# A linear-attention and feed-forward block whose hand-written order and PSUM banks are replaced, tile 1 normalised first and tiles 4 and 5 loaded between the halves of the keys' weight

## The chip, the cores and the metric

The kernel runs on one core of a Trainium2 chip. The core has a matrix engine (TensorE; PE in the profile, its weight loads PEld), a vector engine (VectorE, DVE), a scalar engine (ScalarE, ACT), GpSimd (POOL) and a queue for transfers (SyncE, SP). The metric is the device time of one execution in microseconds (us).

## The reference

The input is one sequence of 2048 rows of 512 bf16 numbers. A pre-normalised linear attention with 32 heads of 16 columns is added to it, and then a pre-normalised feed-forward block with relu of width 1792.

```
h  = x + A(layernorm(x))           # A: linear attention
h2 = h + B(layernorm(h))           # B: relu(h @ w1) @ w2

q, k, v = heads of (x @ wqkv)
phi(t)  = where(t > 0, t + 1, exp(t)) + 1e-6
kv      = sum over s of phi(k)[s, d] * v[s, e]
z       = sum over s of phi(k)[s, d]
o       = (phi(q) @ kv) / (phi(q) @ z + 1e-6)
A       = o.reshape(S, D) @ wo
```

## The kernel before

The 2048 rows are 16 tiles of 128 rows (0 to 15), and four tiles make a chunk of 512 rows (0 to 3). Nothing is scheduled by a compiler: the string `ORDER` is a list of words, the last lines of the kernel read them from left to right, and each word calls one function `op_<name>` with the numbers behind it. An engine runs its instructions in the order in which the words issue them, so the one list is the order of each of the five queues. Where a word on one engine needs the result of another, it waits for it, and everything behind it on that engine waits too.

PSUM has eight banks of 512 f32 columns per partition. The last number of a word of TensorE names the bank that it writes; a later word that writes the same bank waits until the engines that read it are through. `K.4.0` is the keys' product of tile 4 into bank 0.

The words that matter here, in the order in which a tile goes through them:

- `lx` loads tiles of x, `lk`, `lq`, `lv`, `lo`, `l1`, `l2` load weights (lines 201 and 204, SP). `lk.0.2` and `lk.2.2` are the two halves of the keys' weight, 256 KB each; a load of two tiles of x is 256 KB too.
- `S`, `A` (lines 237 and 238, VectorE): statistics of a tile and their sum. `R` (lines 243 and 244, ScalarE): 1/sqrt(variance + eps) as a logarithm and an exponential, of one tile or of several. `N` (line 262, VectorE): the normalised tile into `h_nat`.
- The normalised tile is transposed into `lnT`, in one of two ways. `T` does it on TensorE (line 281) and `E` copies the result out of PSUM on ScalarE (line 291): tiles 0 to 3. `X` does it by a transposing DMA from SP (line 302): tiles 4 to 15. An X needs only its N.
- `K` (line 310): the keys' product, four matmuls of 512 columns, each with a quarter of the weight. `K.t.b.0.2` is its first half, which needs only `lk.0.2`, and `K.t.b.2.2` its second. `F` and `U` (lines 328 and 331, ScalarE) take exp and relu out of PSUM; `M` (line 335, VectorE) clips, `D` (line 338, VectorE) adds, which gives phi(k). `W` does relu and sum in one.
- `G` (line 362): normalised tile times phi(k), summed over all 16 tiles in banks 4 to 7. `za`, `zf`, `z`, `zc`, `zh` make z. `gA` copies G's sum out on ScalarE (line 395), `kv`, `kx`, `m`, `mA` make the matrix that stands for kv and the output weight.
- `Q`, `qF`, `qU`, `qM`, `qD`, `qW`: the same as K to W for the queries of a chunk.
- `dn`, `dnl`, `dnx`: the denominators of a chunk and their reciprocals (line 472, ScalarE). `dt` transposes a tile of these by a DMA (line 491, SP) into `rd`; one tile in each of the first two chunks (2 and 6) goes through TensorE instead (`rt`, then `rv` or `re`). `dm` (line 495, VectorE) multiplies, which needs all four tiles of the chunk.
- `h` (line 505): the attention's output of a tile; `hD` (line 511) adds x. `s`, `a`, `r`, `n`, `x` (`t`, `e` for tile 2) normalise and transpose again.
- `p` (line 521), `pA`, `pD` (lines 527, 532): first feed-forward product and its relu. `f` (line 541) the second, `fo` (line 549) the last sum, `fd` (line 556) the store.
- `warm` and `warmf` (lines 215, 221): matmuls on zeros, whose result nobody reads.

Around the change, the list is this. SP first issues the loads of x and of the keys' weight, which wait for nothing, and then the transposes of tiles 4 to 15, each of which waits for its N. TensorE starts with zeros, transposes tiles 0 to 3 and makes K of them; from G.0 on it goes from K to G to Q without a break in the list. VectorE and ScalarE feed it.

Of the kernel before, what the change touches and what calls it, by code (L numbers as in the profile page):

```python
# [23 lines left out]
A.12 A.13 G.1 R.12.2 K.6.2 K.9.1 M.4.2 S.10 F.6.2 N.12 D.4.2 S.11 A.10 U.6.2 X.8 M.6.2 N.13 G.4 X.12 K.8.0 A.11
R.10.2 S.14 D.6.2 G.5 G.6 X.13 N.10 N.11 S.15 F.8.2 M.8.2 X.11 A.15 U.8.2 A.14 D.8.2 R.14.2 G.7 za.2 za.4 K.12.0
G.9 K.13.1 N.15 N.14 X.10 lq.2.2 K.11.3 F.12.2 K.10.2 M.12.2 U.12.2 F.10.2 masks X.15 X.14 lv.0.2 lv.2.2 l1.0.2
U.10.2 za.6 D.12.2 M.10.2 G.8 za.8 D.10.2 Q.0.1.1 Q.0.0.0 qF.0.0.2 qU.0.0.2 za.10 G.12 K.14.2 K.15.3 Q.0.2.0
za.12 Q.0.3.1 G.13 F.14.2 G.11 qF.0.2.2 l2.10.4 qM.0.0.2 M.14.2 W.14.2 zf.12 G.10 qD.0.0.2 qM.0.2.2 G.14
qU.0.2.2 lo.0.2 z.3.1.14 z.2.1.14 G.15 z.1.1.14 z.0.1.14 qD.0.2.2 zc gA.0.2 gA.2.2 Q.1.0.2 zh dn.0.1 Q.1.1.3
dnl.0 kv.2.7 lo.2.2 kv.1.7 kv.3.7 dnx.0.2.2 qF.1.0.2 kv.0.7 l2.3.4 dnx.0.0.2 Q.1.2.0 l1.2.2 rt.2.6 kx qM.1.0.2  # L30
Q.1.3.1 qF.1.2.2 m.0.4 m.1.5 rv.2 Q.3.1.7 qW.1.0.2 m.3.6 Q.2.3.2 dt.3 qM.1.2.2 mA.0.2 qW.1.2.2 dt.0 dt.1 m.2.5
Q.2.1.4 dn.1.0 mA.2.2 dm.0.0.2 Q.2.2.1 dm.0.2.2 dnl.1 dnx.1.2.2 h.3.6 dnx.1.0.2 h.1.5 rt.6.3 hD.3 qF.2.2.2 dt.7
s.3 re.6 h.0.0 dt.4 qU.2.2.2 hD.1 dt.5 a.3 hD.0 s.1 s.0 a.1 qM.2.2.2 a.0 Q.3.0.6 Q.2.0.3 n.3 h.2.5 n.0 dm.1.0.2
Q.3.3.1 x.3 dm.1.2.2 qF.3.0.2 hD.2 n.1 s.2 Q.3.2.0 qU.2.0.2 qF.2.0.2 h.5.2 h.6.3 a.2 qU.3.0.2 qM.2.0.2 h.4.7 n.2
qF.3.2.2 x.0 qD.2.0.2 t.2.5 qD.2.2.2 hD.4 x.1 hD.6 h.7.4 dn.2.6 hD.5 hD.7 e.2 dnl.2 qM.3.0.2 p.0.0.5 dnx.2.2.2
p.0.13.7 p.0.1.6 p.0.8.2 p.0.9.3 dnx.2.0.2 qD.3.0.2 s.4 l2.7.3 p.0.11.4 pA.0.0.2 dt.11 l2.0.3 dt.9 dt.10 r.0.4
qM.3.2.2 qW.3.2.2 s.6 dt.8 p.0.12.6 s.7 pD.0.12.2 p.0.3.1 p.0.2.0 pA.0.8.2 dn.3.2 p.0.5.7 dnl.3 p.0.4.6 a.7
dm.2.0.2 pA.0.2.2 dnx.3.0.2 dnx.3.2.2 dm.2.2.2 pD.0.4.2 h.9.0 h.8.5 p.0.6.6 p.0.7.7 dt.13 dt.12 s.5 dt.14
p.0.10.3 hD.8 dt.15 s.8 a.6 pD.0.6.2 a.4 pA.0.10.2 n.6 f.1.1.0.7 hD.9 n.7 f.1.1.7.7 s.9 dm.3.0.2 dm.3.2.2 h.11.7
a.5 n.5 h.12.2 h.15.6 h.14.4 fo.1 h.10.5 hD.11 f.0.7.0.7 hD.12 x.6 a.8 h.13.1 a.9 f.3.3.0.7 f.3.3.7.7 x.7 hD.15  # L40
n.4 hD.14 f.0.7.7.7 x.4 f.2.0.0.7 hD.13 fo.3 x.5 p.1.0.6 s.12 s.11 n.8 hD.10 fo.0 p.1.1.7 a.11 fd.0 p.1.5.3 s.10
pD.1.0.2 f.2.0.7.7 a.12 n.12 n.9 s.14 p.1.4.2 n.11 p.1.8.4 fo.2 p.1.3.1 r.4.4 a.10 a.14 p.1.13.7 p.1.2.0
pD.1.4.2 n.10 x.10 x.11 s.13 p.1.7.2 p.1.9.5 p.1.12.6 a.13 pD.1.2.2 s.15 a.15 pD.1.8.2 n.14 pD.1.12.2 p.1.6.1
# [548 lines left out]
```

## Time and profile before

| | |
|---|---|
| time, median of 3 runs | 170.09 us (170.05 to 170.57) |
| span of the profiled execution, first to last instruction | 168.8 us, of 2286 instructions |
| last matmul of that execution ends | 166.14 us after the span's start |
| DMA | 15.49 MB, mean 92 GB/s |

The runs that were timed are other executions than the one that was profiled; for that one the page has the span, to which 1.25 us are missing up to the median.

The page gives for each engine the time in which it was busy. A matmul is shown from its start to a modelled end, and the next one starts before that end; so matmuls that follow each other at full pace look busy throughout, and a short wait between two of them can be hidden in such an overlap. What a group of equal matmuls takes from its start to the start of the next group shows it. The timeline merges neighbouring instructions of one line: start, time from the first start to the last end, engine, line, operation, count, and in brackets the idle time of the engine ahead of it, with what ended it. "Landing" of a DMA counts from its issue to the moment at which all of it has arrived.

### The profile page before, as it was taken

To read this page: it belongs to the slowest core of one execution; us is meant where nothing else is said; L and a number is where in the kernel's file an instruction comes from. 1 tells how busy PE (TensorE), PEld (TensorE's weight loads), DVE (VectorE), ACT (ScalarE), POOL (GpSimd) and SP (SyncE) were. 2 spreads that over 40 slices of the span, in tenths; PEclk is the share of its full clock that TensorE was granted. 3 is DMA by queue.
4 is the path that set the end of the run, shared out by engine and by line. 5 is a ranking of instruction groups with operands and counts; after the bars stand their busy time and mean duration, and the time that the engine had idled before them with its cause. 6 is when DMAs were issued, how large, how long until landed. Compare 5 with 4: busy or idle time off the path is not lost.

```text
span 168.8 us, 2286 instructions
## 1 busy us (share of the span) xinstructions
PE 163.1 (97%) x855; PEld 78.0 (46%) x871; DVE 104.4 (62%) x205; ACT 65.1 (39%) x97; POOL 4.8 (3%) x21
## 2 busy tenths in 40 slices
...
DMA packets 30491, 15.49 MB, mean 92 GB/s; under 512 B 23184, under 2 KB 29328, under 8 KB 30480
## 3 DMA queue, kind: packets, MB, share of 16 engines
...
q8 instruction: 7, 0.11, 0.3%
...
HBM read 7.86 MB, written 2.10 MB: 59 GB/s over the span
## 4 chain that ended last, share of the span: by engine, by line
PE 85%; DVE 7%; DMA 4%; issue 1%; SPq 0%
PE bk L541 29%; PE bk L521 28%; PE bk L505 8%; PE bk L318 8%; PE bk L362 6%; PE bk L310 4%; DVE st L237 3%; DMA x_nat<-in_A_x_dram 2%; DMA lnT<-h_nat 2%; DVE h_nat L262 2%; PE bk L459 1%; DVE eb L335 1%; PE bk L403 1%; PE bk L415 1%; SPq L201 0%
## 5 line engine op out<-in xcount | busy, mean ns | idle before, releaser
L541 PE MATMUL bk<-w_sb,at 128*128 128x512 bf16 (+2 forms) x247 | 50.1, 355 | 0.3
L521 PE MATMUL bk<-lnT,w_sb 128*128 128x512 bf16 x219 | 50.0, 379 | 0.3
L527 ACT ACTIVATE at<-bk 128x1024 bf16<-128x1024 f32 x14 | 14.2, 1023 | 57.4 <-PE bk L521 57.4
L541 PEld LDWEIGHTS <-at 128*128 128x128 bf16 x252 | 23.6, 98 | 25.4 <-ACT at L527 0.3
L549 DVE SCALAR_TENSOR_TENSOR gT<-bk,rstd,h_nat 128x512 bf16<-128x512 f32 (+2 forms) x18 | 12.2, 689 | 35.7 <-PE bk L541 35.6
L521 PEld LDWEIGHTS <-w_sb 128*128 128x128 bf16 x224 | 21.8, 98 | 25.8
L532 DVE TENSOR_SCALAR at<-bk 128x1024 bf16<-128x1024 f32 x14 | 17.1, 1218 | 12.8 <-PE bk L521 12.6
L328 ACT ACTIVATE eb<-bk 128x1024 bf16<-128x1024 f32 (+1 forms) x18 | 16.6, 928 | 6.6 <-PE bk L310 4.8
L310 PE MATMUL bk<-wk_sb,lnT 128*128 128x512 bf16 x63 | 15.3, 380 | 0.4 <-ACT lnT L291 0.3
L505 PE MATMUL bk<-m_sb,pqs 128*128 128x512 bf16 x63 | 15.4, 380 | 0.1
L318 PE MATMUL bk<-lnT,wq_sb 128*128 128x512 bf16 x61 | 15.1, 379 | 0.1
L362 PE MATMUL bk<-at,h_nat 128*128 128x512 bf16 x55 | 13.5, 379 | 0.1
L331 ACT ACTIVATE rb<-bk 128x1024 bf16<-128x1024 f32 (+1 forms) x14 | 12.5, 904 | 0.3 <-PE bk L310 0.3
L511 DVE TENSOR_TENSOR h_nat<-bk,x_nat 128x512 bf16<-128x512 f32 x16 | 10.5, 680 | 2.9 <-PE bk L505 2.9
L237 DVE BATCH_NORM_STATS2 st<-x_nat 128x6 f32<-128x512 bf16 x16 | 10.8, 680 | 2.4 <-DMA x_nat<-in_A_x_dram 2.4
L239 DVE BATCH_NORM_STATS2 st<-h_nat 128x6 f32<-128x512 bf16 x16 | 10.7, 683 | 0.1
L310 PEld LDWEIGHTS <-lnT 128*128 128x128 bf16 x64 | 6.0, 98 | 8.4 <-ACT lnT L291 1.0
L362 PEld LDWEIGHTS <-h_nat 128*128 128x128 bf16 x64 | 6.2, 98 | 7.4 <-issue 0.2
L505 PEld LDWEIGHTS <-pqs 128*128 128x128 bf16 x64 | 5.9, 98 | 7.9 <-DVE pqs L495 1.8
L318 PEld LDWEIGHTS <-wq_sb 128*128 128x128 bf16 x64 | 5.9, 98 | 6.4
L472 ACT ACTIVATE wk_sb<-ld 128x1024 bf16<-128x1024 f32 x8 | 8.1, 1050 | 0.1
L335 DVE TENSOR_SCALAR eb<-eb 128x1024 bf16<-128x1024 bf16 (+1 forms) x18 | 6.8, 383 | 0.9 <-ACT eb L328 0.9
...
## 6 DMA issues: line engine op xcount, KB each, us to landing
...
x_nat<-in_A_x_dram SPq DMA_DIRECT2D x3, 256.0 KB, 4.6
...
wk_sb<-in_A_wqkv_dram SPq DMA_DIRECT2D x2, 256.0 KB, 4.3
wq_sb<-in_A_wqkv_dram SPq DMA_DIRECT2D x2, 256.0 KB, 4.9
```

Source lines behind the costliest of these rows:

```text
L237: op_S = lambda t: nc.vector.bn_stats(out=st[:, t, :], in_=x_nat[:, t, :])
L310: nc.tensor.matmul(bk[:, b, :], lhsT=lnT[c][:, kd, j * P : (j + 1) * P], rhs=wk_sb[:, kd, :], start=(kd == 0), stop=(kd == KD - 1),)
L318: nc.tensor.matmul(bk[:, b, :], lhsT=wq_sb[:, kd, j * P : (j + 1) * P], rhs=lnT[c][:, kd, :], start=(kd == 0), stop=(kd == KD - 1),)
L328: nc.scalar.activation(out=buf(eb, kind, i, n), in_=bank(at_bank[kind, i], n), func=ACT.Exp)
L331: nc.scalar.activation(out=buf(rb, kind, i, n), in_=bank(at_bank[kind, i], n), func=ACT.Relu)
L362: nc.tensor.matmul(bk[:, KD + kd, :], lhsT=ln_nat[:, t, kd * P : (kd + 1) * P], rhs=pk(t)[:, 0, :], start=(t == 0), stop=(t == NT - 1),)
L505: nc.tensor.matmul(bk[:, b, :], lhsT=pqs[:, (c * KD + jb) % NQ, j * P : (j + 1) * P], rhs=m_sb[:, jb, :], start=(jb == 0), stop=(jb == KD ...
L521: nc.tensor.matmul(bk[:, b, cols], lhsT=w1_sb[:, kd, f * P : (f + 1) * P], rhs=lnT[c][:, kd, cols], start=(kd == 0), stop=(kd == KD - 1),)
L527: nc.scalar.activation(out=acts[c % 2][:, f : f + n, :], in_=bank(at_bank["p", c, f], n), func=ACT.Relu)
L532: nc.vector.tensor_scalar(out=acts[c % 2][:, f : f + n, :], in0=bank(at_bank["p", c, f], n), scalar1=0.0, scalar2=None, op0=ALU.max,)
L541: nc.tensor.matmul(bk[:, b, 0 : w * P], lhsT=acts[c % 2][:, f, j * P : (j + 1) * P], rhs=w2_sb[:, f, k * P : (k + w) * P], start=(f == 0), ...
L549: nc.vector.scalar_tensor_tensor(out=o_t[:, t % NO, cols], in0=bk[:, at_bank["f", t, k], 0 : w * P], scalar=rstd2[:, t : t + 1], in1=h_nat ...
```

## The change

Only the string `ORDER` is other. It has the same number of words of every kind, and the same instructions come out, in another order on each engine and with other bank numbers. The first and the last line of it, before and after:

```diff
-const lx.0.1 lx.1.1 warmf.4.3 warm.1.3 S.0 table A.0 R.0.1 S.1 lx.2.2 lk.0.2 warm.1.3 N.0 A.1 S.2 R.1.1 lk.2.2
...
-f.15.5.0.14.2.1 fd.13 fd.14 fd.15.0.2 fo.15.2.1 fd.15.2.1
+lx.0.1 lx.1.1 lx.2.2 lk.0.2 lx.4.2 lk.2.2 lx.6.2 lx.8.4 lv.2.2 table const warmf.4.5 S.0 A.0 S.1 A.1 R.0.1 N.0 R.1.1
...
+f.15.5.0.14.3.1 fo.15.3.1 fd.15.3.1 f.15.4.0.14.2.1 fo.15.2.1 fd.15.2.1
```

As two lines are missing at the head of the file, a line of the kernel after stands two numbers lower than the same line before.

**VectorE, the start of the program.** First the kernel before, from the first statistics on. BN_STATS is S, BN_AGGR is A, TENSOR_SCALAR from x_nat is N.

```order
L237 BN_STATS st<-x_nat 128x6
L238 BN_AGGR mv<-st 128x2
L237 BN_STATS st<-x_nat 128x6
L262 TENSOR_SCALAR h_nat<-x_nat,mv,rstd 128x512
L238 BN_AGGR mv<-st 128x2
L237 BN_STATS st<-x_nat 128x6
L238 BN_AGGR mv<-st 128x2
L237 BN_STATS st<-x_nat 128x6
L238 BN_AGGR mv<-st 128x2
L262 TENSOR_SCALAR h_nat<-x_nat,mv,rstd 128x512 x3
L237 BN_STATS st<-x_nat 128x6 x2
```

The same place after:

```order
L235 BN_STATS st<-x_nat 128x6
L236 BN_AGGR mv<-st 128x2
L235 BN_STATS st<-x_nat 128x6
L236 BN_AGGR mv<-st 128x2
L260 TENSOR_SCALAR h_nat<-x_nat,mv,rstd 128x512 x2
L235 BN_STATS st<-x_nat 128x6
L236 BN_AGGR mv<-st 128x2
L235 BN_STATS st<-x_nat 128x6
L260 TENSOR_SCALAR h_nat<-x_nat,mv,rstd 128x512
L236 BN_AGGR mv<-st 128x2
L235 BN_STATS st<-x_nat 128x6 x2
```

Tile 1 is normalised right behind tile 0 and no longer behind the statistics of tiles 2 and 3; tile 3 comes next, and tile 2 last, behind the statistics of tiles 4 and 5. On TensorE one matmul on zeros that stood ahead of tile 0's transposes goes to a place behind them, tile 1's transposes come ahead of K.0, and tile 3's stand between K.0's halves.

**SP, from the first load to the last transpose of h_nat.** Before (lnT_82, lnT_83, lnT_84 are the chunks 1, 2 and 3 of lnT; a row with x2 or x4 stands for that many DMAs):

```order
L201 DMA x_nat<-in_A_x_dram 128x512 x2
L201 DMA x_nat<-in_A_x_dram 128x1024
L204 DMA wk_sb<-in_A_wqkv_dram 128x2x512 x2
L201 DMA x_nat<-in_A_x_dram 128x1024 x2
L201 DMA x_nat<-in_A_x_dram 128x2048 x2
L204 DMA wq_sb<-in_A_wqkv_dram 128x2x512
L302 DMA_TRANSPOSE lnT_82<-h_nat 128x4x128 x4
L302 DMA_TRANSPOSE lnT_83<-h_nat 128x4x128 x2
L302 DMA_TRANSPOSE lnT_84<-h_nat 128x4x128 x2
L302 DMA_TRANSPOSE lnT_83<-h_nat 128x4x128 x2
L204 DMA wq_sb<-in_A_wqkv_dram 128x2x512
L302 DMA_TRANSPOSE lnT_84<-h_nat 128x4x128 x2
```

After, from the first half of the keys' weight on:

```order
L202 DMA wk_sb<-in_A_wqkv_dram 128x2x512
L199 DMA x_nat<-in_A_x_dram 128x1024
L202 DMA wk_sb<-in_A_wqkv_dram 128x2x512
L199 DMA x_nat<-in_A_x_dram 128x1024
L199 DMA x_nat<-in_A_x_dram 128x2048
L202 DMA wv_sb<-in_A_wqkv_dram 128x2x512
L199 DMA x_nat<-in_A_x_dram 128x2048
L300 DMA_TRANSPOSE lnT_82<-h_nat 128x4x128 x2
L202 DMA wq_sb<-in_A_wqkv_dram 128x2x512
L300 DMA_TRANSPOSE lnT_82<-h_nat 128x4x128 x2
L202 DMA wq_sb<-in_A_wqkv_dram 128x2x512
L300 DMA_TRANSPOSE lnT_83<-h_nat 128x4x128 x2
```

Tiles 4 and 5 of x are loaded between the two halves of the keys' weight. Both halves of the queries' weight now stand between transposes, and half of the values' weight stands ahead of the last four tiles of x. Behind these rows the transposes of chunks 3, 2 and 3 follow, two each, then the remaining loads without one between the later transposes; before, two parts of w2 stood among the transposes of the reciprocals.

**TensorE, in the stretch from tile 6's keys to tile 12's.** In words, since the rows there read alike: before, K.6 K.9 G.4 K.8 G.5 G.6 G.7 K.12; after, K.6 G.4 G.5 K.8 K.9 G.6 K.13 K.12, with tile 8 transposed ahead of tile 9 and tile 13 ahead of tile 12.

More of the change, by code (lines that the diff above doesn't have):

```diff
@@ L24 @@
[L24 to L43, printed above, removed]
@@ new lines @@
+N.1 warm.1.4 T.0.1 E.0 warm.1.7 T.1.3 K.0.4.0.2 S.3 A.3 R.3.1 S.2 N.3 A.2 E.1 R.2.1 masks S.4 S.5 A.4 A.5 N.2 T.3.0
+K.0.4.2.2 E.3 F.0.1 R.4.2 U.0.1 K.1.3.0.2 K.1.3.2.2 warm.1.1 T.2.1 K.3.0 E.2 K.2.2.0.2 K.2.2.2.2 F.3.1 S.6 N.5 M.0.1
+N.4 D.0.1 S.7 M.3.1 A.7 A.6 lx.12.4 X.5 X.4 lq.2.2 U.3.1 R.6.2 U.2.1 F.2.1 U.1.1 F.1.1 D.3.1 S.9 N.7 S.8 A.9 M.2.1 A.8
+R.8.2 N.6 D.2.1 M.1.1 N.9 G.0 G.3 K.5.1 K.4.0 F.4.2 U.4.2 D.1.1 N.8 S.12 M.4.2 S.13 A.12 D.4.2 A.13 X.7 X.6 lq.0.2 X.8
+X.9 R.12.2 G.2 G.1 K.7.2 K.6.1 F.6.2 U.6.2 S.15 N.13 X.13 A.15 S.10 A.10 M.6.2 N.12 D.6.2 S.11 A.11 R.10.2 S.14 N.10
@@ new lines @@
+A.14 N.11 X.12 G.4 G.5 K.8.0 K.9.1 G.6 K.13.3 K.12.2 G.7 F.8.2 R.14.2 U.8.2 U.12.2 F.12.2 za.2 N.15 N.14 M.8.2 D.8.2
+Q.0.1.1 Q.0.0.0 qF.0.0.2 qU.0.0.2 X.10 X.11 X.15 X.14 lo.2.2 l2.3.4 lv.0.2 lo.0.2 l2.0.3 l2.7.3 l1.0.2 l2.10.4 l1.2.2
+K.10.2 K.11.3 za.4 M.12.2 za.6 D.12.2 za.8 G.9 F.10.2 U.10.2 M.10.2 D.10.2 za.10 K.15.1 K.14.0 G.8 F.14.2 M.14.2 za.12
+W.14.2 qM.0.0.2 G.12 Q.0.3.3 Q.0.2.2 G.13 G.10 G.14 G.11 qF.0.2.2 qU.0.2.2 zf.12 z.2.2.14 z.1.2.14 z.3.2.14 z.0.2.14
+G.15 gA.0.2 qD.0.0.2 zc zh qM.0.2.2 qD.0.2.2 Q.1.0.3 gA.2.2 dn.0.1 dnl.0 dnx.0.2.2 Q.1.1.4 kv.3.2 kv.2.2 kv.0.2 kv.1.2
@@ new lines @@
+Q.1.3.1 Q.1.2.0 qF.1.0.2 dnx.0.0.2 kx qM.1.0.2 qW.1.0.2 dt.3 dt.0 dt.1 qF.1.2.2 m.0.6 m.1.7 Q.2.3.2 mA.0.2 rt.2.3
+m.2.5 Q.3.1.4 m.3.6 qM.1.2.2 qW.1.2.2 rv.2 dm.0.0.2 mA.2.2 Q.2.1.7 dn.1.3 Q.2.2.1 dnl.1 dnx.1.0.2 dnx.1.2.2 qF.2.2.2
+qU.2.2.2 dm.0.2.2 h.3.5 hD.3 h.0.3 h.1.0 s.3 hD.0 hD.1 s.0 s.1 a.0 a.3 n.0 n.3 a.1 n.1 rt.6.5 Q.2.0.6 h.2.2 Q.3.3.1
+Q.3.0.3 Q.3.2.0 dt.5 dt.7 dt.4 qF.2.0.2 re.6 qU.2.0.2 dm.1.0.2 dm.1.2.2 h.4.5 h.5.6 h.6.7 hD.2 s.2 a.2 qM.2.0.2 n.2
+qU.3.0.2 qF.3.0.2 qF.3.2.2 t.2.4 qD.2.0.2 qM.2.2.2 hD.6 qD.2.2.2 h.7.2 hD.7 qM.3.0.2 hD.4 x.3 x.0 x.1 e.2 qM.3.2.2
@@ new lines @@
+qD.3.0.2 qW.3.2.2 p.0.3.4 dn.2.7 p.0.2.3 pA.0.2.2 r.0.4 dnl.2 dnx.2.0.2 p.0.6.2 p.0.9.5 p.0.8.4 dn.3.1 pA.0.8.2
+dnx.2.2.2 p.0.7.3 hD.5 s.5 s.6 pD.0.6.2 p.0.10.6 p.0.4.4 p.0.5.5 p.0.1.3 p.0.0.2 s.7 a.6 n.6 s.4 a.4 dt.8 dt.9 dt.11
+dt.10 a.7 pD.0.4.2 a.5 n.7 dm.2.0.2 dm.2.2.2 n.5 p.0.11.7 p.0.12.5 dnl.3 pA.0.0.2 pA.0.10.2 dnx.3.0.2 dnx.3.2.2 r.4.4
+f.0.4.0.7 h.8.1 p.0.13.6 pD.0.12.2 n.4 h.10.3 h.11.0 hD.11 f.1.2.0.7 hD.10 s.10 f.0.4.7.7 f.2.7.0.7 dt.13 dt.14 dt.12
+dt.15 dm.3.0.2 a.10 dm.3.2.2 h.13.6 s.11 hD.8 hD.13 a.11 s.13 x.5 x.7 f.1.2.7.7 fo.1 fd.1 x.4 x.6 h.12.0 h.15.3 a.13
```

22 lines of the change are left out of this document (10 added, 12 removed).

## The prediction

> **What bounds the kernel now.** I read the page's busy times and its chain of work, and then the busy times of stretches.
>
> ```profile
> PE 163.1 (97%) x855; PEld 78.0 (46%) x871; DVE 104.4 (62%) x205; ACT 65.1 (39%) x97; POOL 4.8 (3%) x21
> PE 85%; DVE 7%; DMA 4%; issue 1%; SPq 0%
> ```
>
> ```profile
> 0.00:12.13 12.13, 10.07 (x43) 5.71 (x44) 8.71 (x27) 7.66 (x20) 4.81 (x21) 1.00 0.71 238
> 12.13:49.33 37.20, 36.84 (x225) 17.80 (x228) 32.24 (x67) 27.05 (x39) 0.00 (x0) 1.00 0.68 167
> ```
>
> In the stretches the columns are length, then busy time and count of PE, PEld, DVE, ACT and POOL, granted clock, DMA share and GB/s. TensorE makes 85% of the chain and is busy nearly throughout behind 12.13 us (36.84 of the next 37.20). The change adds and removes no instruction, so only three things can move: when TensorE's unbroken work begins, how long it stands still afterwards, and what lies behind its last matmul. The first stretch, with 2 us of 12 idle, is a chain of VectorE, ScalarE and TensorE.
>
> The pace of unbroken matmuls is in the chain, and the standstills in the timeline:
>
> ```profile
> 129.81 10.14 PE bk L521 x47
> ```
>
> ```profile
> 19.94 1.03 PE L362 MATMUL bk<-at,h_nat 128*128 128x512 bf16 x4
> 21.09 0.55 PEld L310 LDWEIGHTS <-lnT 128*128 128x128 bf16 x4 [0.63 <-DMA lnT<-h_nat]
> 21.10 1.04 PE L310 MATMUL bk<-wk_sb,lnT 128*128 128x512 bf16 x4
> 48.93 0.54 PE L459 MATMUL bk<-zhd,pqT 128*128 128x8 bf16 x16
> 50.25 2.07 PE L505 MATMUL bk<-m_sb,pqs 128*128 128x512 bf16 x8
> 69.81 1.89 PE L521 MATMUL bk<-lnT,w_sb 128*128 128x512 bf16 x8
> 71.62 2.07 PE L505 MATMUL bk<-m_sb,pqs 128*128 128x512 bf16 x8
> ```
>
> 10.14 / 47 gives 0.216 us for a matmul and 0.863 for a group of four. G.4 at 19.94 should end its issue at 20.80, but K.8 starts at 21.10, when X.8 has landed: 0.30 lost. Eight matmuls at full pace take 1.89 (the row at 69.81); the two rows of h take 2.07, so 0.18 is lost in each. Ahead of the first, the small matmuls of dn.1 end their issue at about 49.33 and Q.2.2 would at 50.19, so 0.06 is lost before 50.25; ahead of the second it is 71.62 - (69.81 + 1.73) = 0.08. Together 0.30 + 0.24 + 0.26 = 0.80; the records have little else, so a new order can win **about 0.8 us** behind G.0. The rest has to come from the front.
>
> **The front, step by step.** The rows, in the order in which the walk uses them:
>
> ```profile
> 3.94 0.66 DVE L237 BATCH_NORM_STATS2 st<-x_nat 128x6 f32<-128x512 bf16 x1
> 4.63 0.41 DVE L262 TENSOR_SCALAR h_nat<-x_nat,mv,rstd 128x512 bf16<-128x512 bf16 x1
> 4.82 1.06 PE L215 MATMUL bk<-m_sb 128*128 128x512 bf16 x2
> 4.96 0.18 DVE L238 BATCH_NORM_AGGREGATE mv<-st 128x2 f32<-128x6 f32 x1
> 5.17 0.29 ACT L243 ACTIVATE rstd<-mv,eps 128x1 f32<-128x1 f32 x1 [0.57 <-DVE mv L238]
> 5.49 0.20 ACT L244 ACTIVATE rstd<-rstd 128x1 f32<-128x1 f32 x1
> 5.60 0.70 DVE L237 BATCH_NORM_STATS2 st<-x_nat 128x6 f32<-128x512 bf16 x1 [0.47 <-DMA x_nat<-in_A_x_dram]
> 5.67 0.63 PE L281 MATMUL bk<-ident,h_nat 128*128 128x128 bf16 x4
> 6.34 0.60 ACT L291 ACTIVATE lnT<-bk 128x512 bf16<-128x512 bf16 x1 [0.64 <-PE bk L281]
> 6.99 1.05 PE L310 MATMUL bk<-wk_sb,lnT 128*128 128x512 bf16 x4 [0.26 <-ACT lnT L291]
> 8.24 1.28 DVE L237 BATCH_NORM_STATS2 st<-x_nat 128x6 f32<-128x512 bf16 x2
> 9.43 2.75 PE L310 MATMUL bk<-wk_sb,lnT 128*128 128x512 bf16 x12
> 12.13 1.02 PE L362 MATMUL bk<-pk_lo,h_nat 128*128 128x512 bf16 x4
> ```
>
> A result passes to another engine in about 0.04 us (T.0 ends at 6.30, E.0 starts at 6.34), and VectorE overlaps neighbours by some 0.09 (two S in 1.28).
>
> Tile 0: S.1 ends at 4.60 as before, A.1 now follows, and N.0 runs 4.73 to 5.14, 0.1 later than before. But T.0 stood behind two matmuls on zeros, which issue every 0.43 us (4.82 to 5.67 for two); with one it goes off at 5.25, E.0 runs 5.91 to 6.51, and K.0's first half 6.57 to 7.00. That is 0.42 earlier. Tile 1: A.1 ends at 4.82, R.1 at 5.38 (0.52 from the first start to the last end), N.1 at 5.82, so T.1 fits in ahead of K.0. Tile 3: S.3 5.74 to 6.43, A.3, R.3 to 7.21, N.3 7.25 to 7.65, T.3 at 7.70, and K.0's second half at 7.93 to 8.36. Its weight has moved behind 256 KB of x.
>
> ```profile
> 2.18 0.95 SPq L204 DMA_DIRECT2D wk_sb<-in_A_wqkv_dram  x2
> wk_sb<-in_A_wqkv_dram SPq DMA_DIRECT2D x2, 256.0 KB, 4.3
> ```
>
> The halves were issued from 2.18 and 2.66 and landed 4.3 later, at 6.5 and 7.0; one more place of the same size in the queue is 0.5 to 0.7, so the second lands by 7.7. TensorE is then busy with T.3, which hides it; without that cover it costs what it lands after 7.9.
>
> E.1 is done at 7.72 and K.1 takes 8.36 to 9.22. Tile 2 is the late one: S.4, S.5, A.4, A.5 are ahead of it on VectorE, N.2 runs 9.07 to 9.47, T.2 9.52, K.3 9.75 to 10.61 meanwhile; E.2 waits on ScalarE behind U.0 and ends at 10.70, K.2 takes 10.76 to 11.62. D.0 is ready at 11.26. So **G.0 starts at 11.62 in place of 12.13: 0.51 us won**.
>
> **From G.0 to h.** After G.0, G.3 needs D.3, which VectorE has at 12.58: 0.14 lost. The next points are the transposing DMAs of tiles 4 to 15.
>
> ```profile
> 10.85 14.66 SPq L302 DMA_TRANSPOSE lnT<-h_nat  x10
> lnT<-h_nat SPq DMA_TRANSPOSE x12, 2.5
> ```
>
> ```profile
> 19.27 1.02 ACT L328 ACTIVATE eb<-bk 128x1024 bf16<-128x1024 f32 x1 [0.80 <-PE bk L310]
> 20.34 0.42 DVE L335 TENSOR_SCALAR eb<-eb 128x1024 bf16<-128x1024 bf16 x1
> ```
>
> Issue occupies SP for about 1.2 us of the 2.5 to landing. By the same walk X.5 goes off at 10.44 (before 10.85), X.4 at 11.75 and lands at 14.25, where K.4 wants it at 14.35. X.8 is issued at 16.6 and is wanted at 20.4, so the 0.30 of before is gone even with a load of 256 KB ahead of it. X.9 lands at 20.4 to 21.2 by how much that load holds it up, and is wanted at 21.2: I put 0.1 there. The tight one is X.12. K.6 ends at 18.84, R.12 is ahead of F.6, F.6 ends at 20.12 (1.02), M.6 waits for S.10 and takes 0.42 to 20.88, then comes N.12 to 21.20. X.12 is issued at 21.23 and lands at 23.7; K.12 wants it at 23.85 to 23.95. I count nothing for it, with 0.15 to spare.
>
> Then a chain of waits runs from the last G to h.3:
>
> ```profile
> 39.44 1.02 PE L362 MATMUL bk<-at,h_nat 128*128 128x512 bf16 x4
> 40.07 1.94 ACT L395 ACTIVATE gT<-bk 128x1024 bf16<-128x1024 f32 x2 [2.15 <-PE bk L362]
> 42.35 1.06 ACT L472 ACTIVATE wk_sb<-ld 128x1024 bf16<-128x1024 f32 x1
> 46.53 1.76 SPq L491 DMA_TRANSPOSE rd<-wk_sb  x1
> 49.50 1.29 DVE L495 TENSOR_TENSOR pqs<-pqT,rd 128x1024 bf16<-128x1024 bf16 x2 [1.02 <-DMA rd<-wk_sb]
> ```
>
> gA, dnl, dnx, one qF, the second dnx, two dt, dm: ScalarE, SP and VectorE do them in the same order before and after, from the last G's second matmul on. TensorE's arrival at h.3 moves by -0.51 (front), -0.30 (X.8), +0.14 (G.3) and +0.10 (K.9): 0.57 earlier. The last G, which starts the chain, moves by the same and by +0.20, since two of the four z, which stood behind it, now stand ahead of it (eight small matmuls, 0.1 us): 0.37 earlier, and dm with it. So the stop at h.3 grows from 0.24 to **0.44**. Further on, p.0.3 wants x.1 and e.2 at the moment at which, by the walk, both get there, as dn.2 no longer stands ahead of it: 0.05. At the second stop (h.8 in place of h.9) the chunk's multiplications are there 0.6 before h: its 0.26 go. From chunk 1's p on, every bank is free and every relu done 0.2 us or more ahead, or at the same distance as before.
>
> The end: before, the last group of f is followed by one sum and one small store.
>
> ```profile
> 166.18 0.35 DVE L549 SCALAR_TENSOR_TENSOR gT<-bk,rstd,h_nat 128x128 bf16<-128x128 f32 x1 [0.30 <-PE bk L541]
> ```
>
> After, the same sum and store end it, and the store ahead of it is issued 0.8 earlier: no change.
>
> Sum: front 0.51, standstills of before 0.80 won, standstills of after 0.14 + 0.10 + 0.44 + 0.05 = 0.73 lost: **0.58 us less**. Made against the profiled execution this is a span of 168.2 after 168.8; the median of the timed runs, 170.09, stands 1.25 above that span, and I keep that distance: 169.5.
>
> **The rivals.** *X.12 comes late, and the kernel becomes slower.* Two transposes of before landed late, and the DMA view of two windows, that of X.8's issue and that of X.13's, has their times; in the window behind X.13's issue (22.8 to 22.9 us) stands a packet that is not the kernel's:
>
> ```profile
> lnT<-h_nat SPq DMA_TRANSPOSE x1, 3.4
> lnT<-h_nat SPq DMA_TRANSPOSE x1, 4.1
> q8 instruction: 1, 0.02, 54.8%
> ```
>
> X.13 was issued at 21.1 and took 4.1 instead of 2.5 while 16 KB of instructions were fetched through one of the same DMA engines; it was not wanted soon. After, X.12 is issued at 21.23, and K.12 wants it at 23.9. At 4.1 it lands at 25.3: 1.4 lost, which makes 169.5 + 1.4 = 170.9. It makes the kernel slower than before where the landing takes more than about 3.3. Against it: the fetch follows TensorE's progress, which may come past it a little earlier or stand in front of K.12 until X.12 is there. The Trainium skill ("Runtime: NRT & Kernel Launch", section on instruction fetch) says that the sequencer refills its instructions in blocks of 16 KiB, 256 instructions, through a DMA queue of its own; the packet above is such a block, and by that rule it comes at the same count of TensorE's instructions after, beside X.12, with this rival's 170.9 as the result.
>
> *The gain is eaten at one tight place.* A transpose that lands 0.9 late, as X.8 did (3.4), at K.12 (0.15 to spare), K.9 or p.0.3 costs about 0.7: 170.2, no difference.
>
> *The stops vanish.* If the reciprocals' DMAs run without the delay that they had before (the issue at 46.53 took 1.76 us in place of 1.2, which is 0.56 of the chain), h.3 does not stop: 169.1, and 168.8 if K.9 and G.3 do not either.
>
> *The front does not get earlier*, because N.2, now last of four, or the second half of the weight holds K.2 up to 12.1: 170.0.
>
> **How the numbers follow.** The forecast (169.1 to 169.9) gets 0.42, the late X.12 at its full price 0.17, the gain eaten 0.21, no stops 0.12, no earlier front 0.08. The measurement tells about 0.3%, 0.5 us, from no change, so faster means below 169.58: no stops, and somewhat more than half of the forecast and a little of the others where a row was read 0.1 too dear, 0.44 in all. Slower means above 170.6: the late X.12 and a few of the eaten gains, 0.19. The rest, 0.37, is the same. The range leaves out a tenth at each end: 168.7 to 171.0.
>
> **What would show it.** Right: G.0 in the timeline near 11.6, K.0 in two pieces with T.3 between them, G.3 with a short wait for D.3, no wait for a DMA at K.8, the first h stopped for DVE by about half a microsecond, h.8 not stopped. Wrong: an idle time of TensorE ahead of a group of K from 23 us on with a DMA as its releaser, a first G after 11.9, or a wait among the p and f, where I found none.

## The result, and the profile after

| | before | after |
|---|---|---|
| time, median | 170.09 us (170.0 to 170.57, 5 runs) | 171.54 us (171.1 to 172.61, 5 runs) |
| ratio, 95% interval | | 1.0086, 1.0064 to 1.0107 |
| span of the profiled execution | 168.8 us | 169.7 us |

The kernel became slower by 0.9%, where 0.3% faster was forecast; its time lies above the range. The page of the changed kernel, its busy times and its chain of work, and the busy times of the same two stretches:

```profile
PE 162.5 (96%) x856; PEld 77.4 (46%) x871; DVE 105.2 (62%) x205; ACT 64.5 (38%) x97; POOL 4.7 (3%) x21
...
PE 83%; DVE 8%; DMA 4%; ACT 2%; issue 1%
```

```profile
0.00:11.79 11.79, 9.59 (x43) 5.07 (x44) 8.36 (x26) 7.51 (x19) 4.73 (x21) 1.00 0.73 243
11.79:49.33 37.54, 35.90 (x206) 16.96 (x209) 32.24 (x67) 25.80 (x38) 0.00 (x0) 1.00 0.67 185
```

The front did get shorter (G.0 at 11.79 in place of 12.13). Behind it TensorE is idle for 37.54 - 35.90 = 1.64 us where it was idle for 0.36; at an equal clock, so this is waiting and not a slower engine. The timeline of TensorE from K.8 on shows where (L308 is K, L360 is G; all lines are two lower than before):

```profile
20.56 1.03 PE L308 MATMUL bk<-wk_sb,lnT 128*128 128x512 bf16 x4
21.86 1.04 PE L308 MATMUL bk<-wk_sb,lnT 128*128 128x512 bf16 x4 [0.27 <-DMA lnT<-h_nat]
22.73 1.03 PE L360 MATMUL bk<-at,h_nat 128*128 128x512 bf16 x4
23.59 1.03 PE L308 MATMUL bk<-wk_sb,lnT 128*128 128x512 bf16 x4
25.83 0.81 PE L308 MATMUL bk<-wk_sb,lnT 128*128 128x512 bf16 x3 [1.21 <-DMA lnT<-h_nat]
26.47 0.81 PE L360 MATMUL bk<-at,h_nat 128*128 128x512 bf16 x3
```

The rows are K.8, K.9, G.6, K.13, K.12 (of which one matmul's record is missing) and G.7. At 0.863 for a group, K.9 should start at 20.56 + 0.86 = 21.42 and starts 0.43 later; from K.13's start to G.7's two groups lie, 1.73, and it takes 2.88, so **1.16 us are lost at K.12**. Both wait for a DMA that writes lnT, a transpose. The DMA view, in windows 0.1 us wide, has the causes: the first row is the window of X.12's issue at 21.2, the others are windows at 20.4 and at 23.1 (queue, packets, MB, share of time).

```profile
lnT<-h_nat SPq DMA_TRANSPOSE x1, 4.3
...
q14 instruction: 1, 0.01, 19.3%
...
q8 instruction: 1, 0.02, 79.9%
```

X.12 landed 4.3 us after its issue, not 2.5. While it was in flight, 16 KB of instructions were fetched (23.13 to 24.41 us in the packet's record); X.9, which landed 3.4 after its issue, had an 8 KB packet in it (20.46 to 20.77). The trace keeps sixteen completions for each DMA, as many as the page counts DMA engines. Fifteen of X.12's came 2.27 to 2.43 us after its issue and one at 4.31; of X.9's, fifteen came by 2.53 and one at 3.43. So one of the sixteen parts of each transfer was late, and the others were on time.

Against before's profile, by starts of TensorE's groups: G.0 0.33 earlier; K.8's wait of 0.30 gone; G.3 0.11, K.9 0.43 and K.12 1.16 new; a wait of 0.16 in dn.0 new, the 0.24 at the first h gone; 0.21 at the first p new, the 0.26 at the second h gone. That adds up to 0.94, and the last group of f starts 0.90 later, 166.10 after 165.20.

### The profile page after: what moved, and what is told of

Same layout as the page of the kernel before. It is cut to its first block, busy times and chain, and to the rows that moved or that the text cites. A ratio compares the mean times of both kernels' runs of the same rounds, so it can differ in the third digit from the quotient of the medians.

```text
span 169.7 us, 2286 instructions
## 1 busy us (share of the span) xinstructions
PE 162.5 (96%) x856; PEld 77.4 (46%) x871; DVE 105.2 (62%) x205; ACT 64.5 (38%) x97; POOL 4.7 (3%) x21
## 4 chain that ended last, share of the span: by engine, by line
PE 83%; DVE 8%; DMA 4%; ACT 2%; issue 1%
PE bk L539 28%; PE bk L519 28%; PE bk L503 8%; PE bk L316 8%; PE bk L360 5%; DVE st L235 4%; DMA lnT<-h_nat 3%; PE bk L308 3%; DVE h_nat L260 1%; DMA x_nat<-in_A_x_dram 1%; PE bk L457 1%; DVE mv L236 1%; DVE at L336 1%; DVE eb L333 1%; ACT rb L329 1%
## 5 line engine op out<-in xcount | busy, mean ns | idle before, releaser
L519 PE MATMUL bk<-lnT,w_sb 128*128 128x512 bf16 x219 | 49.5, 379 | 0.3
L308 PE MATMUL bk<-wk_sb,lnT 128*128 128x512 bf16 x63 | 15.6, 380 | 1.5 <-DMA lnT<-h_nat 1.5
L503 PE MATMUL bk<-m_sb,pqs 128*128 128x512 bf16 x62 | 15.3, 379 | 0.1
L241 ACT ACTIVATE rstd<-mv,eps 128x2 f32<-128x2 f32 (+2 forms) x14 | 4.1, 295 | 25.7 <-DVE mv L238 19.6
L360 PE MATMUL bk<-at,h_nat 128*128 128x512 bf16 x55 | 13.5, 379 | 0.1
L308 PEld LDWEIGHTS <-lnT 128*128 128x128 bf16 x64 | 5.7, 98 | 9.2 <-DMA lnT<-h_nat 2.9
L360 PEld LDWEIGHTS <-h_nat 128*128 128x128 bf16 x64 | 6.2, 98 | 7.4 <-issue 0.2
L503 PEld LDWEIGHTS <-pqs 128*128 128x128 bf16 x64 | 6.2, 98 | 7.3 <-DVE pqs L493 0.4
```

The lines of the kernel that those rows point to most:

```text
L308: nc.tensor.matmul(bk[:, b, :], lhsT=lnT[c][:, kd, j * P : (j + 1) * P], rhs=wk_sb[:, kd, :], start=(kd == 0), stop=(kd == KD - 1),)
L360: nc.tensor.matmul(bk[:, KD + kd, :], lhsT=ln_nat[:, t, kd * P : (kd + 1) * P], rhs=pk(t)[:, 0, :], start=(t == 0), stop=(t == NT - 1),)
L503: nc.tensor.matmul(bk[:, b, :], lhsT=pqs[:, (c * KD + jb) % NQ, j * P : (j + 1) * P], rhs=m_sb[:, jb, :], start=(jb == 0), stop=(jb == KD ...
L519: nc.tensor.matmul(bk[:, b, cols], lhsT=w1_sb[:, kd, f * P : (f + 1) * P], rhs=lnT[c][:, kd, cols], start=(kd == 0), stop=(kd == KD - 1),)
```

## The experiments

Theory F: packets of instructions, fetched through one of the DMA engines that a transpose uses, hold that transpose up, and the new order stands where that is waited for. Rival A: the loads of the queries' weight, which now stand between the transposes, hold them up. Rival B: the order itself is too tight there (X.12 is issued late, and whatever is mended opens the next stop).

**e1: the kernel before, profiled again.** No edit.

> The kernel before, profiled a second time; nothing is changed. Theory F (instructions fetched through one of the 16 DMA engines delay the transposes in flight): the fetches come at the same counts of instructions again, 8 KB near 19.5 us and 16 KB near 22.9 us, X.8 takes about 3.4 us and K.8 stops for about 0.3, X.13 about 4.1 and stops nobody. If the lateness of X.8 in the first profile was chance, K.8 does not stop, and the span is about 0.3 to 0.5 shorter than 168.84. The time less the span should be near 1.8 us as in the runs of the changed kernel; if it is 1.25, the changed kernel also lost half a microsecond outside of its span.

One run: 170.03 us with a span of 168.3. X.8 landed after 3.46 with an 8 KB packet at 19.53, X.13 after 3.86 with the 16 KB at 22.16, and K.8 stopped for 0.34: the lateness is no chance, it has the same places as in the first profile. What the second profile does not have is lost time in the two rows of h; they run at full pace there (L503 in this file is L505 of the first profile):

```profile
50.18 1.89 PE L503 MATMUL bk<-m_sb,pqs 128*128 128x512 bf16 x8
71.28 1.89 PE L503 MATMUL bk<-m_sb,pqs 128*128 128x512 bf16 x8
```

In the first profile both took 2.07. That execution was the slower one, by 0.5 us of span: time less span is 1.7 here and 1.7 to 1.84 in the five runs of the changed kernel, so 168.84 belongs to about 170.6 and not to the median.

**e2: K.12 one group later.**

```diff
-G.6 K.13.3 K.12.2 G.7
+G.6 G.7 K.13.3 K.12.2
```

> The changed kernel with G.7 ahead of K.13 and K.12 on TensorE, nothing else moved; K.12 is wanted 0.86 us later. Theory F, and rival B (X.12 is issued too late for this order): K.12's stop falls from 1.16 to about 0.3, the time from 171.5 to 170.7, still above before. Rival A (the loads of the queries' weight between the transposes delay them) says the same of this run. If the time stays at 171.5, the stop at K.12 is not what costs, and something further on waits instead (h.3, p.0.3).

171.0 us, ratio 1.0045 (1.0025 to 1.0064). X.12 landed after 4.24, and K.12 stopped for 0.38. The time fell by 0.5 and not by 0.86; K.10 now waited 0.46 for the banks that K.12's results leave later. Both theories F and B had said so. The run agrees that the wait at K.12 is paid, but does not give its exact size: in the profiled execution, 171.55 and thus above the median, the loads of x landed up to 0.9 later than in the changed kernel, X.5 took 3.90 behind them, and K.5 waited 0.87 for it.

**e3: fewer instructions in TensorE's program** (14: 864 weight loads in the records in place of 871, each with its matmul).

```diff
-warmf.4.5 ... warm.1.4 ... warm.1.7 ... warm.1.1
+warmg.2.5
```

> The changed kernel with fewer instructions on TensorE ahead of T.3: three matmuls on zeros are gone and four others are replaced by two longer ones, which is about 8 rows of TensorE's program, nearly one group. Theory F: the 16 KB of instructions are fetched about 0.8 us later by TensorE's progress, at 23.9 to 24.2 us in place of 23.13, when X.12, issued at 21.2, has landed at 23.7; K.12 does not stop (under 0.2), X.9's lateness of 0.9 stays, since the 8 KB at 20.5 are another engine's, and the time falls by about 1.1, to 170.4. Rival A and rival B: nothing of this touches the loads or the order, X.12 lands at 25.5 again, and the time stays at 171.5 (or moves by what the front loses without these matmuls, at most 0.3).

171.8 us, 1.0082 (1.0058 to 1.0106): a miss for theory F as it was put. The fetch near 23 us did not move, 22.87, and X.12 landed after 4.11 again. The last fetch of the program did: it came 1.42 us ahead of the last group of f in the changed kernel and 0.08 behind it here, 1.5 us later. There it hit the last stores. Their median to landing, in the DMA view of 164.7 to 166.5 us, is first that of e3 and then that of the changed kernel:

```profile
out_dram<-gT SPq DMA_DIRECT2D x2, 128.0 KB, 3.1
```

```profile
out_dram<-gT SPq DMA_DIRECT2D x3, 128.0 KB, 2.2
```

The last store was issued 0.58 after its sum was done, in place of 0.03, so that the end came 0.2 later although the last matmuls stood 0.43 earlier. So the last fetch moved the way that the count says, but by more: 842 weight loads had started ahead of it in the changed kernel and 853 here, which with 7 taken away is a place 18 later in the list. Near 23 us it was still open whether the count decides (94 loads ahead of the fetch there, 87 here).

**e4: no load between the transposes.**

```diff
-lx.12.4 X.5 X.4 lq.2.2 ... X.7 X.6 lq.0.2 X.8
+lx.12.4 lq.2.2 lq.0.2 X.5 X.4 ... X.7 X.6 X.8
```

> The changed kernel with both loads of the queries' weight moved ahead of X.5 on SP, so that no load stands between the transposes any more. Rival A: X.9 and X.12 land in 2.5, both stops go (0.43 and 1.16), and the time falls by 1.5 to 170.0. Theory F: X.9 is issued up to 1.2 earlier and lands in time, so K.9's 0.43 goes, but X.12 is issued at 21.2 as before and the 16 KB fetch falls into it: K.12 still stops, for about 1.1 to 1.5 (TensorE gets there earlier by 0.43), and the time stays within 0.4 of 171.5. Rival B: as theory F for the stop, but X.12 itself takes 2.5.

171.72 us, 1.0075 (1.0047 to 1.0102). X.9 landed in 2.48, ahead of the 8 KB, and K.9 did not stop; X.12, with no load near it, took 3.56 around the fetch at 23.19. Rival A falls for X.12. The loads that moved cost as much elsewhere: the weight's second half came late (first row), X.5 behind the loads too (second), and K.12 still waited 0.56 (third).

```profile
8.94 1.46 PE L308 MATMUL bk<-wk_sb,lnT 128*128 128x512 bf16 x6 [0.88 <-DMA wk_sb<-in_A_wqkv_dram]
...
14.89 1.90 PE L308 MATMUL bk<-wk_sb,lnT 128*128 128x512 bf16 x8 [0.52 <-DMA lnT<-h_nat]
...
25.82 1.04 PE L308 MATMUL bk<-wk_sb,lnT 128*128 128x512 bf16 x4 [0.40 <-DMA lnT<-h_nat]
```

**e5: K.12 two groups later, with room behind it.**

```diff
-G.6 K.13.3 K.12.2 G.7 ... Q.0.1.1 Q.0.0.0 ... K.10.2 K.11.3 ... G.9 ... K.14.0 G.8
+G.6 G.7 K.13.3 ... Q.0.1.1 K.12.2 U.12.2 F.12.2 Q.0.0.0 ... G.9 G.8 K.10.2 K.11.3 ... K.14.0
```

> The changed kernel with K.12 two groups later on TensorE (G.7 ahead of K.13, Q.0.1 between K.13 and K.12) and with G.9 and G.8 moved ahead of K.10, which in e2 waited 0.46 for the banks that K.12's exponential and relu release late. K.12 is wanted at 26.2. Theory F: X.12 still lands between 25.1 and 26.1, 1.1 to 1.8 late, but nobody waits for it; K.12 and K.10 stop for less than 0.1 each, the time falls by 1.16, to 170.4, which is no difference from before (170.1 to 170.25). Rival B (the order as such is too tight, whatever is mended opens the next stop): the stop moves to Q.0.0, K.10 or K.15, and the time stays above 171.

171.71 us, 1.0099 (1.0075 to 1.0122). X.12 took 4.07 and nobody waited for it, but the gain was given back: with K.10, K.11, K.15 and K.14 later, the phi of tiles 14 and 15 came late for G.14 (0.74) and the sums for z by another 0.34.

```profile
35.64 1.89 PE L360 MATMUL bk<-at,h_nat 128*128 128x512 bf16 x8
38.10 1.89 PE L360 MATMUL bk<-at,h_nat 128*128 128x512 bf16 x8 [0.57 <-DVE at L341]
```

This is what rival B says, though of another order: to put K.12 late is no remedy.

**e6: 46 instructions more ahead of K.0's second half**, with the order of everything else as it was.

```diff
-warmf.4.5 ... warm.1.4 ... T.3.0
+warmf.2.5 warms.17.5 ... warms.3.4 ... warms.8.5 T.3.0
```

`warms` is the matmul on zeros with 64 columns.

> The changed kernel with 46 more instructions on TensorE ahead of K.0's second half: two of the four long matmuls on zeros and one short one are replaced by 20 tiny ones, and 8 tiny ones fill the idle time ahead of T.3. Nothing else is touched; X.12 is issued when it was. Theory F: the 16 KB fetch comes 46 rows, some 5 us, earlier, at 17.2 to 18.2 us in place of 23.1, where no transpose but lq.0.2's load and the start of X.8 are in flight; X.12 takes 2.5, K.12 does not stop (under 0.1; K.9's 0.43, from another engine's 8 KB, stays), and the time falls by 1.0 to 1.2, to 170.4; up to 0.3 of it may be lost where the tiny matmuls delay T.0 or T.3, or where a fetch 5 us earlier than before meets another DMA. Rival A and rival B: X.12 lands at 25.5 and K.12 stops for 1.1 again, 171.5. In e3 the fetch near 23 us did not move with 14 rows less; if it does not move here with 46 rows more, its place does not follow the count of TensorE's instructions, and theory F has to do without that.

The fetch came at 17.53 us, where 17.2 to 18.2 was forecast, and X.12 landed in 2.48. But lq.0.2 and X.8, which were in flight now, were hit: 4.1 and 4.8 us (X.8 had the 8 KB packet of 20.14 in it as well). The DMA view of X.8's issue (17.2) and of 17.5 to 17.6, and the timeline of K.8:

```profile
lnT<-h_nat SPq DMA_TRANSPOSE x1, 4.8
...
q8 instruction: 1, 0.02, 90.0%
```

```profile
22.02 1.90 PE L308 MATMUL bk<-wk_sb,lnT 128*128 128x512 bf16 x8 [1.18 <-DMA lnT<-h_nat]
```

K.8 lost 1.34, K.12 nothing, and the time stayed at 171.68 (1.0116, 1.0081 to 1.0152). The expected 170.4 was a miss, since X.8 was not seen as a victim. The stop went where the fetch went.

**e7: e5 with three more places relieved** (lq.0.2 behind X.13, lv.2.2 loaded late, dn.2 ahead of p.0.3).

```diff
-X.7 X.6 lq.0.2 X.8 ... N.13 X.13 A.15
+X.7 X.6 X.8 ... N.13 X.13 lq.0.2 A.15
-lx.8.4 lv.2.2 table ... p.0.3.4 dn.2.7
+lx.8.4 table ... lv.2.2 lo.2.2 ... dn.2.7 p.0.3.4
```

> e5 with three more places relieved: lq.0.2 is issued behind X.13, where SP waits for N.12 anyway (X.9 goes off 0.65 earlier, at 17.7, lands at 20.2 and is out of the way of the 8 KB fetch at 20.5; K.9's 0.43 goes), lv.2.2 is loaded at 29 us in place of 4.6 (tile 12's load and X.5 come earlier; K.5 gets 0.3 to spare), and dn.2 stands ahead of p.0.3 again (0.21 goes). Theory F: 171.5 - 1.16 - 0.43 - 0.21 = 169.7, some 0.4 below before, which a ratio of 0.9975 says, faster than both. Rival B: the stops move on, 170.5 or more.

172.4 us, 1.013 (1.0108 to 1.0152), a miss. X.9 landed in 2.47 and K.9 did not stop, as forecast. But the 16 KB (22.16 to 23.94 here) now fell on lq.0.2 as well, which took 4.58, as long as X.12 behind it; the row is Q.0.1, which needs lq.0.2 and lost 0.73:

```profile
25.55 1.04 PE L316 MATMUL bk<-lnT,wq_sb 128*128 128x512 bf16 x4 [0.57 <-DMA wq_sb<-in_A_wqkv_dram]
```

G.14 and z lost what they lost in e5. In place of the 0.21 at the first p, dn.2, which stands ahead of it now, lost 0.25 ahead of its first matmul and 0.56 in its middle, where it waited for a sum on VectorE that was done at 63.17.

**e8: the fetch moved to where no transpose is.** 75 tiny matmuls in place of four long ones put 134 more instructions ahead of T.0; they take 4.03 us where the long ones took 3.78. The load lv.2.2 is moved back too.

```diff
-warmf.4.5 ... lx.8.4 lv.2.2 table ... lo.2.2
+warms.75.5 ... lx.8.4 table ... lv.2.2 lo.2.2
```

> The changed kernel with its four long matmuls on zeros replaced by 75 tiny ones, which take the same 3.8 us in e6's measure (0.05 us each) and put some 134 rows more into TensorE's program ahead of T.0; and with lv.2.2 loaded at 29 us in place of 4.6, to leave the room in the loads' queues that the fetch will take. Theory F: the 16 KB come at 7.5 to 9.5 us, when only loads of x are in flight; X.12 takes 2.5, K.12 does not stop, K.9's 0.43 stays (another engine's 8 KB, at 20.5), and no other transpose is late between 10 and 27 us: 171.5 - 1.16 = 170.4. If a load of x is held up by the fetch, G.0 may come up to 0.5 later. Rival B (the order is too tight whatever is mended): a new stop of 0.7 or more elsewhere before the last G, and the time stays above 171.2.

170.38 us, 1.0016 (1.0001 to 1.0031), where 170.4 was forecast. The packet came at 10.19 us, a little behind the forecast's 7.5 to 9.5. The DMA view of X.12's issue (21.2) and of 10.15 to 10.25, and the timeline from K.9 on (K.9, G.6, then K.13 and K.12 in one row at full pace):

```profile
lnT<-h_nat SPq DMA_TRANSPOSE x1, 2.5
...
q8 instruction: 1, 0.02, 63.7%
```

```profile
21.88 1.04 PE L308 MATMUL bk<-wk_sb,lnT 128*128 128x512 bf16 x4 [0.33 <-DMA lnT<-h_nat]
22.75 1.03 PE L360 MATMUL bk<-at,h_nat 128*128 128x512 bf16 x4
23.62 1.89 PE L308 MATMUL bk<-wk_sb,lnT 128*128 128x512 bf16 x8
```

X.12 was issued at the same 21.2 as in the changed kernel, behind the same work, and it is in time; K.9's wait for X.9 (8 KB at 20.46 again) stayed, at 0.50. The other thing that this run changes, the place of lv.2.2, is not the reason: e7 loads it late too, and X.12 took 4.58 there. So neither the order nor the loads make K.12 late, and F is what is left.

**e9: e8, with lq.0.2 behind X.13.** The edit is the first pair of e7.

> e8 with lq.0.2 issued behind X.13 in place of ahead of X.8, as in e7, where the 16 KB fetch made it land 4.6 late and Q.0.1 wait for it; here no fetch is near. Theory F: X.9 is issued at 17.7, lands at 20.2, ahead of the 8 KB, K.9 does not stop: 171.5 - 1.16 - 0.43 = 169.9, no difference from before or a little faster (170.0 to 170.25). Rival B as in e8.

170.53 us, 1.0028 (1.0013 to 1.0043): half a miss. X.9 landed in 2.50 and K.9 did not stop, but lq.0.2 directly ahead of X.12 put that off by 0.3 and made it take 2.96, and K.12 lost 0.65. So a load does hold up the transpose behind it, by 0.5 us: this much of rival A is true.

**e10: the kernel before, with its fetch moved on a transpose that is wanted soon.**

```diff
-warmf.4.3 warm.1.3 ... warm.1.3 ... warm.1.3
+warmf.2.3 warms.17.3 warms.4.3 ... warms.4.3 ... warms.4.3
```

> The kernel before, not the changed one, with some 44 rows more of TensorE's program ahead of K.0 (two long and three short matmuls on zeros replaced by 33 tiny ones); its order is untouched. Theory F: its 16 KB fetch, which falls on X.13 at 22.2 to 22.9 us and hurts nobody, comes at 17 to 18 us, on X.9 or the end of X.6, whose tiles TensorE wants within 0.3 to 0.8 us of their landing: K.6 or K.9 stops for 0.4 to 1.2 and the time rises from 170.1 to between 170.4 and 171.2. If it is the new order and not the fetch that is slow, the time stays at 170.1 (or moves by what the front does, at most 0.2).

172.34 us, 1.0129 (1.0097 to 1.016): before's own order gets slower than the changed one. The fetch came at 17.58, X.9 landed after 4.03 and K.9 lost 1.33. The DMA view of X.9's issue (16.0) and of 17.5 to 17.7, and K.6 and K.9 in the timeline:

```profile
lnT<-h_nat SPq DMA_TRANSPOSE x1, 4.0
...
q8 instruction: 1, 0.02, 27.7%
```

```profile
17.85 1.03 PE L308 MATMUL bk<-wk_sb,lnT 128*128 128x512 bf16 x4
20.05 1.04 PE L308 MATMUL bk<-wk_sb,lnT 128*128 128x512 bf16 x4 [1.17 <-DMA lnT<-h_nat]
```

The third fetch moved too, from about 63 to 59.98 us, onto the transposes of chunk 0's normalised rows (4.09 and 3.32 in place of 2.44 and 2.47), and the first p lost 0.58; that stop, and the larger one at K.9, are why even the profiled run, 171.31 and the fastest of its six, lies above the forecast's 171.2. What the others lose beyond it is open.

**e11: e8, with lq.0.2 behind X.12.**

```diff
-X.7 X.6 lq.0.2 X.8 ... N.11 X.12 G.4
+X.7 X.6 X.8 ... N.11 X.12 lq.0.2 G.4
```

> e8 with lq.0.2 issued behind X.12 in place of ahead of X.8 (in e9, ahead of X.12, it took X.12's place in the queues and cost 0.65 at K.12). Theory F: X.9 is issued at 17.7 and lands at 20.2, ahead of the 8 KB, K.9 does not stop; X.12 is issued at 21.2 and lands at 23.7, K.12, wanted at 24.0, does not stop; lq.0.2 lands at 25.5, and Q.0.1 wants it at 25.7. 170.4 - 0.45 = 169.9, between 0 and 0.3% below before. If lq.0.2 lands 0.3 or more later than that, Q.0.1 stops for it and the time is 170.2.

169.93 us, 0.9979 (0.9963 to 0.9995), as forecast: faster than both kernels. K.8, K.9, G.6, K.13, K.12 and G.7 follow each other without a wait (X.12 landed at 23.49, K.12 began at 23.84), and the stretch from G.0 has no idle time left that the busy times show; by the groups' starts G.3 still waits 0.12 and dn.0 0.16:

```profile
20.39 1.89 PE L308 MATMUL bk<-wk_sb,lnT 128*128 128x512 bf16 x8
22.11 1.03 PE L360 MATMUL bk<-at,h_nat 128*128 128x512 bf16 x4
22.98 1.89 PE L308 MATMUL bk<-wk_sb,lnT 128*128 128x512 bf16 x8
24.70 1.03 PE L360 MATMUL bk<-at,h_nat 128*128 128x512 bf16 x4
```

```profile
11.64:49.33 37.69, 37.68 (x232) 18.21 (x231) 33.30 (x70) 27.09 (x40) 0.00 (x0) 1.00 0.70 192
```

**e12: the control.** The kernel before with e8's 75 tiny matmuls (`warmf.4.3` becomes `warms.75.3`).

> A control: the kernel before, with its four long matmuls on zeros replaced by the same 75 tiny ones as in e8. Theory F: its 16 KB fetch goes from 22.5 to about 10 us; X.13, on which it fell, lands in 2.5 in place of 3.9, but nobody wanted it; K.8's 0.33 (the other engine's 8 KB) stays; the time stays at 170.0 (169.7 to 170.3). If 134 more instructions, or the later places of the following fetches, give something by themselves, the time falls here by as much as from the changed kernel to e8, to 169.0, and e8 says nothing on X.12.

170.52 us, 1.0019 (1.0005 to 1.0034), 0.2 above the forecast's upper end. X.13 landed in 2.40 and nothing was gained by it. K.4 waited 0.32 for X.4, which landed 0.17 later than in e1, and K.8 only 0.10 in place of 0.34 behind it. More was lost further on: the second 16 KB packet, now at 51.33 us, fell on dt.7 (2.98 in place of 2.47), dt.4 and dt.5 were issued 0.55 later behind it, and TensorE lost 0.46 around h.5 and h.4. The tiny matmuls are no gain by themselves, so e8's gain came from X.12.

The transposes that these theories are about, from the records of the issues, landings and packets (us):

| run | transpose: issue, landing, time | packet: start to end | landing behind the packet's end |
|---|---|---|---|
| after | X.9: 18.38, 21.81, 3.43 | 8 KB, 20.46 to 20.77 | 1.04 |
| after | X.12: 21.25, 25.55, 4.31 | 16 KB, 23.13 to 24.41 | 1.15 |
| e1 | X.8: 17.58, 21.04, 3.46 | 8 KB, 19.53 to 20.00 | 1.04 |
| e1 | X.13: 21.06, 24.92, 3.86 | 16 KB, 22.16 to 23.21 | 1.70 |
| e2 | X.12: 21.81, 26.05, 4.24 | 16 KB, 22.92 to 24.47 | 1.58 |
| e3 | X.12: 21.02, 25.13, 4.11 | 16 KB, 22.87 to 23.80 | 1.33 |
| e4 | X.12: 22.22, 25.78, 3.56 | 16 KB, 23.19 to 24.30 | 1.47 |
| e5 | X.12: 21.03, 25.10, 4.07 | 16 KB, 22.95 to 23.89 | 1.21 |
| e6 | X.8: 17.18, 21.98, 4.80 | 16 KB, 17.53 to 18.97, and 8 KB, 20.14 to 20.80 | 3.00 and 1.17 |
| e7 | X.12: 21.59, 26.18, 4.58 | 16 KB, 22.16 to 23.94 | 2.23 |
| e10 | X.9: 15.98, 20.01, 4.03 | 16 KB, 17.58 to 18.47 | 1.54 |
| e8, e11 | X.12: 21.22 and 21.10, 23.71 and 23.49, 2.49 and 2.40 | none | |

In e6 and e7 the load lq.0.2, issued just ahead, was held up by the same 16 KB packet. In e3 and e5, as in the changed kernel, only one of X.12's sixteen completions was late; in the rows of e1, e2, e4, e7 and e10 all sixteen were late together, and why is open.

## Why the prediction was wrong

**The step that failed is X.12, counted at nothing with 0.15 to spare.** Its issue was worked out rightly (21.23; it was 21.25), and K.12 wanted it at 24.45, 0.5 later than the walk had, mostly because K.9 had stopped by then. Its duration was not worked out: the 2.5 of the page's median was put in, although the prediction's own rows had a transpose in flight at the same time of the program, X.13, at 4.1, and the packet beside it. That was made a rival with a chance of 0.17. The reason given against it, that the fetch follows TensorE's progress and might come by earlier, had no row behind it: TensorE's list has as many instructions ahead of that point as before (93 weight loads ahead of the fetch before, 94 after), and it came there at about the same time, so the fetch was to be expected there again, and what was in flight there was now the transpose wanted next. The rival's mechanism, its place and its price (1.4 lost; 1.16 measured) were right; that its 170.9 is still 0.6 below the measured time lies for the most part in the 0.5 by which the first profile was a slow execution. As e6, e8 and e10 show, the fetch moves with the count of instructions, so this rival was the case to expect, and not one of 0.17. The Trainium skill ("Runtime: NRT & Kernel Launch", section on instruction fetch) gives blocks of 256 instructions for the rule that was cited there. The trace agrees: 748 weight loads, each with its matmul, lie between the first and the last 16 KB packet of the changed kernel, six blocks of about 249 instructions. And in e6, 46 instructions more moved the last fetch by 5.0 us, 46 times the 0.108 that is half of a matmul's 0.216.

The other terms:

- K.9, put at 0.10, lost 0.43. It took two things together. The load ahead, which was thought of, put X.9's issue off to 18.38 (17.60 in e11, without it), and so the 8 KB packet, which in before fell on X.8, fell into X.9 and cost it 0.9 us. Without the load X.9 landed ahead of the packet or within 0.2 of its start, in time (e4, e7, e9, e11); with the load, but with the packet only 0.2 ahead of the landing, it was in time too (e2). K.8's wait was rightly expected to go, but the delay behind it had only changed its victim.
- The front, 0.51, gave 0.33. TensorE's steps came in the order of the walk, but from T.3 on 0.2 later (7.90 in place of 7.70). In e2 and e5, with the same front, G.0 started at 11.76 and 11.58, which brackets the forecast's 11.62: the size was right, within what the front varies from one execution to the next. Tile 0 of x landed at 3.28 here, 3.13 in e2 and 3.04 in e5, which may be the cause and is not shown to be.
- G.3, 0.14: it was 0.11.
- h.3, expected to wait 0.44, did not wait at all:

```profile
50.75 0.81 PE L316 MATMUL bk<-lnT,wq_sb 128*128 128x512 bf16 x3
51.40 2.75 PE L503 MATMUL bk<-m_sb,pqs 128*128 128x512 bf16 x12
```

  The chain of waits got shorter by 0.4 (from gA's start to dm 9.03 in place of 9.43), because the reciprocals' transposes ran at their normal pace: the view of the tile rd between 40 and 55 us has, first before and then after (least, median, most from issue to landing):

```profile
DMA to landing us min/median/max: 2.4/2.7/3.6
```

```profile
DMA to landing us min/median/max: 2.4/2.5/2.7
```

  The 8 KB packet at 47.2, in the middle of them before, came at 44.4. This is the condition of the rival "the stops vanish", met through the same cause. It need not be the whole cause: e1 has that packet at 47.16, its chain takes 9.13, and h.3 does not wait there either. But dn.0 stopped for 0.16 in its middle, which the walk had missed: its third weight load, at 42.61, waited for the queries' sum on VectorE, done at 42.57.
- p.0.3, put at 0.05, lost 0.21: x.1 landed at 62.16, and h.7 was through at 62.20, but the first matmul followed the landing only 0.25 later (0.05 at K.8 before). A tie in a walk is no zero.
- Of the 0.80 that before was to lose, two times 0.18 were in that one execution and not in e1's. And the distance of 1.25 from span to median was no constant of the kernel: it is 1.66 to 1.89 in every run that has both. The forecast span of 168.2 should have been read as 170.0, no difference, even without X.12.

With the measured terms the walk closes: 168.84 - 0.33 - 0.80 + 0.11 + 0.43 + 1.16 + 0.16 + 0.21 = 169.78, for 169.7 in the profile.
